# Half of the second channel product's sums into x, moved from VectorE to a ScalarE copy and a GpSimd DMA that adds in SBUF

## The chip, the cores and the metric

The kernel runs on one core of a Trainium2 chip. Its engines are TensorE (PE in the profile), VectorE (DVE), ScalarE (ACT), GpSimd (POOL) and SyncE (SP, which here issues the loads and stores). The metric is device time in microseconds; the median of three runs of the kernel before is 458.24 us (458.11 to 458.42).

## The reference

Three blocks run one after the other on a batch of 2, a sequence of 768 and a width of 512. The first is a linear attention with a decay, of 8 heads:

```
state = gamma * state + k_t v_t^T
y_t   = scale * q_t state
```

The second mixes along the sequence through a rank of 32 and then runs a channel network of width 2048:

```
u   = x + (x^T U V)^T
x   = u + relu(u @ w_ch1) @ w_ch2
```

The third is a gated block, with a normalised half and a 768 x 768 spatial matrix:

```
h      = relu(x @ w_in);  u, v = halves of h
v_s    = w_spatial @ normalise(v) + b_spatial
output = (u * v_s) @ w_out
```

The change touches the second block's last line: the sum of `relu(u @ w_ch1) @ w_ch2` into x.

## The kernel before

x lies in SBUF, feature by token: for each batch b a tile of 128 partitions with 4 feature blocks d and 768 tokens, cut into two halves h of 384. Products are made with three PE instructions each ("triple"): every operand is split into a high part and the low part that is left over (`hw` and `lw` of a weight, `f..` and `a` of data), and high times high, high times low and low times high are added in PSUM.

The channel network goes through the 2048 hidden features in 8 steps m of 256, for each b; `ch1` makes the hidden features of a step and `ch2` multiplies them with the step's rows of w_ch2. `ch2` makes 8 products of 128 x 384 for each (m, b): for h in 0, 1 and d in 0 to 3, two triples into one PSUM bank named acc, which DVE then adds to x (line 760). PE's program runs ch1 of the next (m, b) interleaved with ch2 of this one. In the first two steps (m below MS = 2) ch1 is four plain products (banks c); from the third on it is a Strassen-like scheme of seven (`quad`, banks q), whose operands are differences of blocks of u (`differ`, tiles s0..t, and `split`, tiles f0..t). These differences read x before the sums of ch2 have changed it, so a sum may have to wait for them.

The weights come as 64-bit numbers and are made into float32 by `convert` (two ACT conversions yw and tw, two DVE instructions on rw, one POOL addition on rw) and split by `parts` (ACT cast hw, subtraction lw on DVE or POOL).

Nothing of the order is written by hand. Every piece of work is handed to `Plan.op` with the engines that may do it and a cost for each, the tiles that it reads and writes, and a key (a due time). `arrange` then plays the program through: at each step it takes the operation that can start first by its costs, engine by engine, and fixes its place in that engine's queue; `settle` repeats this in 15 rounds, in which each key is moved half way to the latest start that `latest` works out. So one operation with another engine or cost can shift the order in other places. Tiles come from pools (`POOLS`) with a fixed number of buffers, of which `ps` are PSUM's 8 banks; an operation cannot be placed before there is a buffer. The engines run their queues strictly in that order and wait for each other by semaphores.

Names that the rows use: t are transposes of x, xtok their copies, g and gt the rank-32 product of the second batch and its copy, hu its product with V, which is added to x (line 509).

Of the kernel before, what the change touches and what calls it, by code (L numbers as in the profile page):

```python
# [8 lines left out]
F32 = mybir.dt.float32  # L9
# [12 lines left out]
P = 128  # L22
# [4 lines left out]
T = S // 2  # L27
# [10 lines left out]


class Op:  # L40
    __slots__ = ("key", "eng", "fn", "bufs", "deps", "outs", "need", "start", "end", "seq", "size", "cost")


class Plan:
# [13 lines left out]
        self.ops, self.last, self.readers = [], {}, {}  # L58
        self.key, self.pace = 0.0, 1.0

    def op(self, eng, fn, r=(), w=(), key=None, size=0):

        o = Op()
        o.key, o.eng, o.fn, o.size = (self.key if key is None else key), dict(eng), fn, size
        deps, bufs = {}, []
        for tok in list(r) + list(w):
            b = tok if isinstance(tok, Buf) else tok[0]
            if isinstance(b, Buf) and b not in bufs:
                bufs.append(b)
                b.left += 1  # L70
        for tok in r:
            if tok in self.last:
                deps[self.last[tok].seq] = self.last[tok]
        for tok in w:
            for x in self.readers.get(tok, ()):
                deps[x.seq] = x
            if tok in self.last:
                deps[self.last[tok].seq] = self.last[tok]
        for tok in w:
            self.last[tok] = o  # L80
            self.readers[tok] = []
        for tok in r:
            if tok not in w:
                self.readers.setdefault(tok, []).append(o)
        o.deps = list(deps.values())
        o.key = max([o.key] + [x.key + 1e-6 for x in o.deps])
        o.bufs, o.outs, o.need, o.seq = bufs, [], len(o.deps), len(self.ops)
        for d in o.deps:
            d.outs.append(o)
        self.ops.append(o)  # L90
        return o

    def arrange(self, sizes):
# [54 lines left out]
        while given < len(order):  # L148
            best, moved = None, False
            for e in self.ENGINES:  # L150
                can = []
                for o in cands[e]:
                    t0 = room(o)
                    if t0 is not None:
                        can.append((o.seq, o, t0) + span(o, e, t0))
                if not can:
                    continue
                low = min(c[3] for c in can) + SLACK.get(e, 30.0)
                for _, o, t0, st, en in sorted(can, key=lambda c: c[0]):
                    if st > low:  # L160
                        continue
                    if len(o.eng) > 1:
                        x = min(o.eng, key=lambda x: span(o, x, t0)[1] + BIAS[x] + harm(o, x) + sum(c.eng[x][0] for c in cands[x] if c.seq < o.seq and len(c.eng) == 1 and c.key > o.key - NEAR))
                        for z in [z for z in o.eng if z != x]:
                            cands[z].remove(o)
                            del o.eng[z]
                        moved = moved or x != e
                        if x != e:
                            continue
                    if best is None or st < best[0]:  # L170
                        best = st, en, o, e
                    break
            if best is None and moved:
                continue
            if best is None:
                left = sorted({o.seq: o for e in cands for o in cands[e]}.values(), key=lambda o: o.seq)
                raise RuntimeError("nothing can start: " + "; ".join(f"{o.key:.1f} {[b.name for b in o.bufs]}" for o in left[:5]) + f" {({p: (len(s), [b.name for b in queue[p][head[p]:head[p] + 3]]) for p, s in slots.items()})}")
            st, en, o, e = best
            given += 1
            for x in o.eng:  # L180
                cands[x].remove(o)
            if e in "DE":
                free[e] = st + 430.0
                en = dma = max(st + 1500.0 + o.size / 210.0, dma + o.size / 360.0)
            else:
                free[e] = en
                if e == "P":
                    tiles = o.eng[e][1]
                elif o.eng[e][1]:
                    port = [en - 20.0, e]  # L190
            o.start, o.end, o.cost, o.eng = st, en, o.eng[e], e
            for b in o.bufs:
                if b not in placed:
                    placed.add(b)
                    heapq.heappop(slots[b.pool])
                    while head[b.pool] < len(queue[b.pool]) and queue[b.pool][head[b.pool]] in placed:
                        head[b.pool] += 1
                b.left -= 1
                b.end = max(b.end, en + self.LAG[e])
                if not b.left:  # L200
                    heapq.heappush(slots[b.pool], b.end)
            for x in o.outs:
                x.need -= 1
                if not x.need:
                    add(x)

    def latest(self):

        end = max(o.end for o in self.ops)
        free = {e: end + 1e3 for e in self.ENGINES}  # L210
        tiles, late = None, {}
        for o in sorted(self.ops, key=lambda o: (-o.start, -o.seq)):
            e, cost = o.eng, o.cost
            t = end
            for x in o.outs:
                if e != "P" or x.eng != "P":
                    t = min(t, late[x] - self.LAG[e] - (45.0 if x.eng == "G" and e != "G" else 0.0))
                else:
                    t = min(t, late[x])
            if e in "DE":  # L220
                t = min(t - 1500.0 - o.size / 210.0, free[e] - 430.0)
            else:
                t = min(t, free[e] + self.OVER[e]) - cost[0]
                if e == "P":
                    t -= 130.0 if tiles not in (None, cost[1]) else 0.0
                    tiles = cost[1]
            free[e] = late[o] = t
        return late
# [64 lines left out]

NM = NF // 2

POOLS = {"a": 36, "w": 24, "raw": 2, "y": 2, "t": 2, "r": 6, "st": 6, "s": 2, "g": 2, "sm": 2, "ps": 8}
SLACK = {'P': 0.0, 'V': 100.0, 'A': 150.0, 'G': 300.0, 'D': 30.0}
BIAS = {'V': 0.0, 'G': 0.0, 'A': -200.0}
HARM = 10.0
# [13 lines left out]
INPLACE = lambda m, b, i, h: False  # L313

MS = 2
SEQ = [(m, b) for m in range(NM) for b in range(B)]

STEP = {n: 6 * pe(n)[0] / 1000 for n in (T, DM // 2)}
# [5 lines left out]
def tile_kernel(ctx: ExitStack, tc: tile.TileContext, a, out: bass.AP):  # L324
# [425 lines left out]
    def ch2(m, b):  # L750
        for h in range(2):
            for d in range(ND):
# [3 lines left out]
                for i in range(2):  # L756
                    wh, wl = W["tile", "w2", 2 * m + i]
                    x = A[m, b, i, h]
                    triple(o, i == 0, i == 1, T, lambda wh=wh, sl=sl: wh.t[:, sl], lambda wl=wl, sl=sl: wl.t[:, sl], lambda x=x: x.t[:, 0, :], lambda x=x: x.t[:, 1, :], [wh, wl, (x, 0), (x, 1)])
                op({"V": vps(T)}, lambda E, o=o, v=xs(b, d, h): E.tensor_add(v, o.t, v), r=[o, ("X", b, d, h)], w=[("X", b, d, h)])  # L760

# [279 lines left out]
```

## Time and profile before

| | us |
|---|---|
| median of 3 runs | 458.24 |
| the profiled execution | 458.86 |
| its span, first to last instruction | 457.1 |
| PE busy | 450.3 (99%) |
| DVE busy | 394.8 (86%) |
| ACT busy | 252.7 (55%) |
| POOL busy | 106.6 (23%) |

The granted clock of PE is 1.00 over the span. Matmuls overlap: a 128 x 384 one is listed with 334 ns, but the next starts about 0.17 us after it, so PE that is busy without a gap is PE that starts one after the other. In the timelines a row can hold several instructions of one form in a row ("x2"), and the square bracket at its end says how long the engine stood idle before it and for whom.

### The profile page before, as it was taken

How to read it: one execution, taken by the hardware profiler on the slowest of the kernel's cores; microseconds unless marked ns; L12 is line 12 of the kernel's file. 1: busy time of each engine (PE TensorE's matmuls, PEld its weight loads, DVE VectorE, ACT ScalarE, POOL GpSimd, SP SyncE). 2: the span in 40 equal slices, each digit the busy share in tenths (PEclk: the TensorE clock that was granted, in tenths of full speed). 3: DMA queues.
4: the chain of work that ended last, by engine and by line, in shares of the span. 5: the costliest groups of instructions: out<-in, count | busy, mean ns of one | idle time of the engine just before them, and what ended most of it. 6: DMA issues, size and time to landing. Idle time of an engine off the chain costs nothing.

```text
span 457.1 us, 8432 instructions
## 1 busy us (share of the span) xinstructions
PE 450.3 (99%) x3245; PEld 437.3 (96%) x3245; DVE 394.8 (86%) x836; ACT 252.7 (55%) x518; POOL 106.6 (23%) x100
## 2 busy tenths in 40 slices
PE   9999989999999999999999999999999999999996
PEld 5888869999999999999999999999999999999996
DVE  2766989899998999999789788899998899999943
ACT  2366785635665665666355444557657778443510
POOL 3045454444324221331031012101310001240000
PEclk9999999999999999999999999999999999999999
DMA  8994521412324132334122112100004220000033
GB/s 298 400 397 175 180 93 47 138 47 92 100 87 139 52 133 92 93 93 138 47 74 66 46 47 69 36 1 1 1 1 138 94 93 1 1 2 0 0 139 138
DMA packets 14296, 43.34 MB, mean 95 GB/s; under 512 B 1713, under 2 KB 2609, under 8 KB 14257
## 3 DMA queue, kind: packets, MB, share of 16 engines
q1 hardware_dynamic: 14112, 42.80, 27.6%
q8 instruction: 25, 0.41, 0.4%
q14 instruction: 15, 0.11, 0.1%
q10 hardware_dynamic: 144, 0.02, 0.0%
HBM read 39.67 MB, written 3.15 MB: 94 GB/s over the span
## 4 chain that ended last, share of the span: by engine, by line
PE 95%; DVE 3%; ACT 1%; issue 0%; ACTq 0%
PE acc L336 29%; PE pz L336 11%; PE c L336 7%; PE sc L336 3%; PE x L336 3%; PE idle L336 1%; PE ds L336 1%; DVE x L509 1%; PE t L478 1%; DVE x L462 1%; PE qu11c L336 0%; PE qu11d L336 0%; PE qo11d L336 0%; PE qo11c L336 0%; PE qo11a L336 0%; PE qo10d L336 0%
## 5 line engine op out<-in xcount | busy, mean ns | idle before, releaser
L336 PE MATMUL acc<-a,hw 128*128 128x384 f32 x512 | 129.8, 334 | 0.0
L336 PEld LDWEIGHTS acc<-a,hw 128*128 128x128 f32 x512 | 92.4, 188 | 0.0
L336 PE MATMUL acc<-a,lw 128*128 128x384 f32 x256 | 85.5, 334 | 0.0
L760 DVE TENSOR_TENSOR x<-acc,x 128x384 f32<-128x384 f32 x128 | 69.5, 550 | 8.2 <-PE acc L336 8.0
L576 POOL TENSOR_TENSOR rw<-rw,tw 128x512 int32<-128x512 int32 x32 | 44.1, 1383 | 109.8 <-DVE rw L574 104.2
L336 PEld LDWEIGHTS acc<-a,lw 128*128 128x128 f32 x256 | 48.1, 188 | 0.0
L733 ACT ACTIVATE y<-y 128x384 f32<-128x384 f32 x36 | 18.9, 526 | 40.5 <-DVE y L732 40.4
L571 ACT ACTIVATE yw<-raww 128x512 f32<-128x512 f32 x32 | 21.5, 675 | 18.4 <-DVE rw L574 17.7
L572 ACT ACTIVATE tw<-raww 128x512 int32<-128x512 uint32 x32 | 21.5, 673 | 3.3 <-POOL rw L576 3.3
L735 DVE TENSOR_TENSOR a<-y,a 128x384 fp32r<-128x384 f32 x36 | 20.7, 574 | 2.8 <-ACT a L734 2.4
L574 DVE SCALAR_TENSOR_TENSOR rw<-yw,rw 128x512 uint32<-128x512 uint32 x32 | 22.2, 702 | 0.0
L427 DVE SCALAR_TENSOR_TENSOR pt<-sc,scales,shared 128x384 f32<-128x384 f32 x21 | 12.0, 609 | 9.5 <-PE sc L336 9.5
L336 PE MATMUL pz<-hws,vn 128*128 128x384 f32 x72 | 19.1, 335 | 0.0
L734 ACT CAST a<-y 128x384 fp32r<-128x384 f32 x36 | 18.5, 514 | 1.0
L336 PE MATMUL pz<-ws,vn 128*128 128x384 f32 x108 | 19.0, 334 | 0.0
L336 PEld LDWEIGHTS pz<-ws,vn 128*128 128x128 f32 x108 | 18.8, 188 | 0.0
L585 DVE TENSOR_TENSOR lw<-rw,hw 128x512 fp32r<-128x512 f32 x19 | 17.7, 931 | 0.4 <-ACT hw L584 0.4
L576 POOL TENSOR_TENSOR rwo<-rwo,two 128x512 int32<-128x512 int32 x4 | 5.2, 1293 | 54.8 <-DVE rwo L574 54.8
L336 PE MATMUL c<-f00b,hw 128*128 128x384 f32 x64 | 16.6, 340 | 0.0
L336 PE MATMUL c<-f01b,hw 128*128 128x384 f32 x64 | 16.2, 334 | 0.0
L584 ACT CAST hw<-rw 128x512 fp32r<-128x512 f32 x20 | 12.4, 620 | 5.1 <-POOL rw L576 5.0
L336 PEld LDWEIGHTS sc<-q,k 64*128 64x128 f32 x192 | 12.4, 193 | 2.8 <-issue 1.4
(1007 smaller groups left out, 1242.4 us busy)
## 6 DMA issues: line engine op xcount, KB each, us to landing
raww<-in_w SPq DMA_DIRECT2D x32, 512.0 KB, 3.5
q<-in_qT SPq DMA_DIRECT2D x8, 384.0 KB, 7.9
k<-in_kT SPq DMA_DIRECT2D x8, 384.0 KB, 7.7
kk<-in_k SPq DMA_DIRECT2D x8, 384.0 KB, 7.7
v<-in_v SPq DMA_DIRECT2D x8, 384.0 KB, 7.8
raws<-in_ws SPq DMA_DIRECT2D x6, 384.0 KB, 3.0
out_y<-out SPq DMA_DIRECT2D x6, 384.0 KB, 2.3
rawwu<-in_wu SPq DMA_DIRECT2D x4, 512.0 KB, 3.5
```

Source lines behind the costliest of these rows:

```text
L336: nc.tensor.matmul(o, l, r, start=start, stop=stop, skip_group_check=True)
L427: op({"V": (611, False)}, lambda E, pt=pt, x=sc[e], m=m: E.scalar_tensor_tensor(pt(), x.t, m, tri(), ALU.mult, ALU.mult), r=[sc[e], "sc", ...
L571: op({"A": c}, lambda E: E.activation(y.t, words(1).bitcast(F32), AF.Copy, scale=2.0 ** -112), r=whole, w=[y])
L572: op({"A": c}, lambda E: E.activation(t.t, words(0), AF.Copy, scale=2.0 ** -29), r=whole, w=[t])
L574: op({"V": vss(n)}, lambda E: E.scalar_tensor_tensor(r.t, y.t.bitcast(U32), 0x80000000, r.t, ALU.bitwise_and, ALU.bitwise_or), r=[y, r], w ...
L576: op({"G": gss(n)}, lambda E: E.tensor_tensor(o().bitcast(I32), r.t.bitcast(I32), t.t, ALU.add), r=[r, t], w=[tok])
L584: op({"A": acp(DM)}, lambda E: E.copy(h.t, f(r.t)), r=[r], w=[h])
L585: op({"V": vss(DM), "G": gss(DM)}, lambda E: E.tensor_sub(l.t, f(r.t), f(h.t)), r=[r, h], w=[l])
L733: op({"A": (525, False)}, lambda E: E.activation(y[0](), y[0](), AF.Relu), r=[y[1]], w=[y[1]])
L734: op({"A": acp(T)}, lambda E: E.copy(t.t[:, 0, :], y[0]()), r=[y[1]], w=[(t, 0)])
L735: op({"V": vss(T), "G": gss(T)}, lambda E: E.tensor_sub(t.t[:, 1, :], y[0](), f(t.t[:, 0, :])), r=[y[1], (t, 0)], w=[(t, 1)])
L760: op({"V": vps(T)}, lambda E, o=o, v=xs(b, d, h): E.tensor_add(v, o.t, v), r=[o, ("X", b, d, h)], w=[("X", b, d, h)])
```

## The change

In `ch2`, for all steps but the last (m below 7), the sums of the feature blocks d = 1 and d = 3 are no longer a DVE addition. ACT copies the PSUM bank into an SBUF tile sg (pool of two), and POOL issues a DMA from sg to that part of x which adds to what is there. That is 4 of the 8 sums of each (m, b), 56 in all. The planner counts the DMA with 1000 ns on POOL and with 2500 ns more until its result is there (`tail`). The pool st, of which the quads take their temporary tiles, goes from 6 buffers to 5.

```diff
@@ Plan.op, Plan.arrange, Plan.latest
-    def op(self, eng, fn, r=(), w=(), key=None, size=0):
+    def op(self, eng, fn, r=(), w=(), key=None, size=0, tail=0.0):
...
+            en += o.tail
             o.start, o.end, o.cost, o.eng = st, en, o.eng[e], e
...
-                t = min(t, free[e] + self.OVER[e]) - cost[0]
+                t = min(t - o.tail, free[e] + self.OVER[e]) - cost[0]
...
-POOLS = {"a": 36, "w": 24, "raw": 2, "y": 2, "t": 2, "r": 6, "st": 6, "s": 2, "g": 2, "sm": 2, "ps": 8}
+POOLS = {"a": 36, "w": 24, "raw": 2, "y": 2, "t": 2, "r": 6, "st": 5, "s": 2, "g": 2, "sg": 2, "sm": 2, "ps": 8}
...
+SENT = [(d, h) for d in (1, 3) for h in range(2)]
+SEND = 1000.0, False
...
@@ ch2
-                op({"V": vps(T)}, lambda E, o=o, v=xs(b, d, h): E.tensor_add(v, o.t, v), r=[o, ("X", b, d, h)], w=[("X", b, d, h)])
+                v, tok = xs(b, d, h), ("X", b, d, h)
+                if m < NM - 1 and (d, h) in SENT:
+                    sg = Buf("sg", [P, T], F32, f"sg{m}{b}{h}{d}")
+                    op({"A": aps(T)}, lambda E, o=o, sg=sg: E.copy(sg.t, o.t), r=[o], w=[sg])
+                    op({"G": SEND}, lambda E, sg=sg, v=v: E.dma_start(v, sg.t[:], accum_op=ALU.add), r=[sg, tok], w=[tok], tail=2500.0)
+                else:
+                    op({"V": vps(T)}, lambda E, o=o, v=v: E.tensor_add(v, o.t, v), r=[o, tok], w=[tok])
```

The order of PE's instructions stays nearly as it was (four groups of three change places with a neighbour, and around 55 to 66 us the first c products take their tiles in another order); SP's stays the same; from about 300 us on all five queues are the same. The queues of DVE, ACT and POOL are new between about 54 and 300 us.

The first place is ACT's queue around gt, the copy that PE's product hu reads (c_929 and c_932 are the same first c product of the channel network, x_95 and x_98 batch 0 of x, x_96 and x_99 batch 1). Before:

```order
L571 ACTIVATE yw_960<-raww_847 128x512
L729 ACTIVATE a_989<-c_929 128x384
L537 CAST f00t_992<-s00t_962 128x384
L571 ACTIVATE yw_996<-raww_902 128x512
L465 COPY gt_1000<-g_964 128x128
L584 CAST hw_1008<-rw_885 128x512
```

And with the change:

```order
L574 ACTIVATE yw_958<-raww_850 128x512
L732 ACTIVATE a_993<-c_932 128x384
L574 ACTIVATE yw_997<-raww_905 128x512
L468 COPY gt_999<-g_968 128x128
L587 CAST hw_1007<-rw_888 128x512
```

The cast of f00t, which waits for the difference s00t of DVE, no longer stands ahead of gt.

The second place is DVE's queue from there to lw, the low half of the weight tile with which PE goes on after hu. Before:

```order
L730 SCALAR_TENSOR_TENSOR a_989<-c_929,a_989 128x384
L509 TENSOR_TENSOR x_96<-hu_1002,x_96 128x384
L509 TENSOR_TENSOR x_96<-hu_1003,x_96 128x384
L574 SCALAR_TENSOR_TENSOR rw_994<-yw_960,rw_994 128x512
L585 TENSOR_TENSOR lw_1033<-rw_885,hw_1008 128x512
```

With the change:

```order
L733 SCALAR_TENSOR_TENSOR a_993<-c_932,a_993 128x384
L512 TENSOR_TENSOR x_99<-hu_1001,x_99 128x384
L577 SCALAR_TENSOR_TENSOR rw_965<-yw_958,rw_965 128x512
L588 TENSOR_TENSOR lw_1027<-rw_888,hw_1007 128x512
L512 TENSOR_TENSOR x_99<-hu_1002,x_99 128x384
```

One sum of hu stands behind lw instead of ahead of it.

And PE, directly behind hu, has before:

```order
L336 MATMUL c_1037<-f00b_845,hw_859 128x384
L336 MATMUL c_1037<-f00b_845,lw_889 128x384
L336 MATMUL c_1045<-f00b_683,hw_1008 128x384
L336 MATMUL c_1045<-f00b_683,hw_1008 128x384
L336 MATMUL c_1045<-f00b_683,lw_1033 128x384
```

With the change:

```order
L339 MATMUL c_1037<-f00b_686,hw_1007 128x384
L339 MATMUL c_1037<-f00b_686,hw_1007 128x384
L339 MATMUL c_1037<-f00b_686,lw_1027 128x384
L339 MATMUL c_1037<-f00b_689,hw_1007 128x384 x2
L339 MATMUL c_1037<-f00b_689,lw_1027 128x384
```

The triple with the weight tile that was there already (hw_859, lw_889) has gone further back, so lw is asked for three products earlier.

The third place is POOL's queue where the moved sums begin (steps (0, 0) and (0, 1), 70 to 100 us in the trace of before). With the change:

```order
L767 DMA x_98<-sg_1162 128x384
L579 TENSOR_TENSOR rw_1177<-rw_1177,tw_1033 128x512
L579 TENSOR_TENSOR rw_1182<-rw_1182,tw_1120 128x512
L541 TENSOR_TENSOR f00t_1184<-s00t_1169,f00t_1184 128x384
L767 DMA x_98<-sg_1263 128x384
L579 TENSOR_TENSOR rw_1257<-rw_1257,tw_1224 128x512
L579 TENSOR_TENSOR rw_1280<-rw_1280,tw_1246 128x512
L767 DMA x_98<-sg_1336 128x384
L535 TENSOR_TENSOR s01t_1371<-x_99,s01t_1352 128x384
L767 DMA x_99<-sg_1393 128x384
L767 DMA x_98<-sg_1212 128x384
L767 DMA x_99<-sg_1437 128x384
```

The DMAs stand between the additions of the weight conversion, of which before had these in a row with differences and splits. The DMA of sg_1212, the second copy that ACT makes, comes fifth: it changes a part of x that the planned differences read until then.

## Rows read from the trace of the kernel before

**Rows 1.** Windows: busy us of PE, PEld, DVE, ACT, POOL; PEclk, DMA share, GB/s

```profile
0.00:54.00 54.00, 52.46 (x828) 42.09 (x828) 34.87 (x66) 29.19 (x60) 20.96 (x30) 1.00 0.81 297
54.00:64.00 10.00, 8.32 (x103) 5.96 (x95) 8.89 (x16) 6.99 (x15) 3.65 (x4) 1.00 0.28 78
64.00:292.00 228.00, 228.00 (x1315) 228.00 (x1316) 207.32 (x407) 128.15 (x245) 63.22 (x50) 1.00 0.27 85
292.00:440.00 148.00, 148.00 (x933) 148.00 (x932) 138.11 (x340) 86.46 (x196) 18.77 (x18) 1.00 0.10 34
440.00:457.10 17.10, 13.56 (x79) 13.23 (x77) 5.58 (x10) 1.93 (x4) 0.00 (x0) 0.99 0.32 124
```

**Rows 2.** Line 760: ns min/median/max, first and last start in us

```profile
L760 DVE TENSOR_TENSOR x<-acc,x x128: 541/549/560, 73.6 to 321.8; 128x384 f32<-128x384 f32 x128
```

**Rows 3.** PE's waits over the span: us in total, times, longest

```profile
PE hu L336 <- ACT gt L465: 1.2, 1, 1.2
...
PE c L336 <- DVE lw L585: 0.5, 1, 0.5
```

**Rows 4.** Timeline of PE from 57 us: start, us, instructions, idle before

```profile
57.83 1.52 PE L336 MATMUL g<-xtok,ust 128*32 128x128 f32 x48
...
60.77 1.57 PE L336 MATMUL hu<-vst,gt 32*128 32x384 f32 x16 [1.16 <-ACT gt L465]
...
64.00 0.45 PE L336 MATMUL c<-f00b,lw 128*128 128x384 f32 x1 [0.52 <-DVE lw L585]
```

**Rows 5.** Timeline of ACT, 55 to 61.5 us

```profile
57.98 0.46 ACT L729 ACTIVATE a<-c 128x384 fp32r<-128x384 f32 x1
59.24 0.51 ACT L537 CAST f00t<-s00t 128x384 fp32r<-128x384 f32 x1 [0.80 <-DVE s00t L532]
59.89 0.67 ACT L571 ACTIVATE yw<-raww 128x512 f32<-128x512 f32 x1
60.47 0.25 ACT L465 COPY gt<-g 128x128 f32<-128x128 f32 x1
```

**Rows 6.** Timeline of POOL, 57.2 to 64.5 us

```profile
57.39 1.41 POOL L576 TENSOR_TENSOR rw<-rw,tw 128x512 int32<-128x512 int32 x1 [2.96 <-DVE rw L574]
```

**Rows 7.** Timeline of DVE, 54.5 to 64.5 us

```profile
57.57 1.64 DVE L532 TENSOR_TENSOR s00t<-x 128x384 f32<-128x384 f32 x1
...
61.72 1.02 DVE L509 TENSOR_TENSOR x<-hu,x 128x384 f32<-128x384 f32 x2 [1.10 <-PE hu L336]
62.66 0.68 DVE L574 SCALAR_TENSOR_TENSOR rw<-yw,rw 128x512 uint32<-128x512 uint32 x1
63.26 0.69 DVE L585 TENSOR_TENSOR lw<-rw,hw 128x512 fp32r<-128x512 f32 x1
```

**Rows 8.** Timeline of PE, 68.9 to 70.6 us

```profile
69.48 0.51 PE L336 MATMUL c<-f01b,hw 128*128 128x384 f32 x2
```

**Rows 9.** A costly group of the page: busy us, mean ns, idle before

```profile
L576 POOL TENSOR_TENSOR rw<-rw,tw 128x512 int32<-128x512 int32 x32 | 44.1, 1383 | 109.8 <-DVE rw L574 104.2
```

**Rows 10.** Line 465, the copies of a PSUM bank on ACT

```profile
L465 ACT COPY xtok<-t x13: 462/480/491, 20.4 to 56.9; 128x384 f32<-128x384 f32 x13
```

**Rows 11.** DMA issues: KB each, median us to landing

```profile
q<-in_qT SPq DMA_DIRECT2D x8, 384.0 KB, 7.9
...
out_y<-out SPq DMA_DIRECT2D x4, 192.0 KB, 1.9
bb<-in_bsp SPq DMA_DIRECT2D x2, 192.0 KB, 2.9
```

**Rows 12.** Timeline of PE, 80.3 to 86.3 us, the last matmuls of two products

```profile
80.75 0.33 PE L336 MATMUL acc<-a,lw 128*128 128x384 f32 x1
...
84.91 0.33 PE L336 MATMUL acc<-a,lw 128*128 128x384 f32 x1
```

**Rows 13.** Timeline of PE, 73.5 to 75.3 us, the end of a product

```profile
74.51 0.33 PE L336 MATMUL acc<-a,lw 128*128 128x384 f32 x1
```

**Rows 14.** Timeline of DVE, 82.5 to 83.5 us, its sum

```profile
82.89 1.01 DVE L760 TENSOR_TENSOR x<-acc,x 128x384 f32<-128x384 f32 x2
```

More of the change, by code (lines that the diff above doesn't have):

```diff
@@ L40 @@
 class Op:
-    __slots__ = ("key", "eng", "fn", "bufs", "deps", "outs", "need", "start", "end", "seq", "size", "cost")
+    __slots__ = ("key", "eng", "fn", "bufs", "deps", "outs", "need", "start", "end", "seq", "size", "cost", "tail")
 class Plan:
@@ L86, in op @@
         o.key = max([o.key] + [x.key + 1e-6 for x in o.deps])
-        o.bufs, o.outs, o.need, o.seq = bufs, [], len(o.deps), len(self.ops)
+        o.bufs, o.outs, o.need, o.seq, o.tail = bufs, [], len(o.deps), len(self.ops), tail
         for d in o.deps:
```

## The prediction

> **What bounds the kernel now.** I read the table of windows first. In it the reader is to see that from 64 to 440 us TensorE (PE) is busy the whole time, 228.00 of 228.00 us and 148.00 of 148.00 us, while VectorE (DVE) is busy 91% and 93% of the same stretches [rows 1]. The second channel product, whose sums the change moves, begins in the first of them (its 128 sums start between 73.6 and 321.8 us, 112 of them in the seven steps that the change touches) [rows 2]. So DVE work taken out there is worth nothing by itself: PE is what ends last, and no instruction of PE goes away. PE has room only before 64 us, where 8.32 of 10 us are busy between 54 and 64, and in the tail after 440 us.
>
> Second I read PE's waits. After 54 us two are listed: 1.2 us for a ScalarE (ACT) copy that makes gt, and 0.5 us for a DVE subtraction that makes lw, the low half of a weight tile [rows 3]. The timeline of PE shows both in their place: g ends at 57.83 + 1.52 = 59.35, hu starts only at 60.77, and the c product that needs lw goes on at 64.00 [rows 4]. From there on PE never waits until the tail. A microsecond that PE gains before 64 us is therefore carried to the end, unless the changed work makes PE wait later.
>
> **The change part by part.**
>
> *The order on ACT around gt.* The planner puts everything in a new order, and the first difference that matters lies ahead of the first moved sum. Before, ACT's queue held a cast of f00t in front of gt [rows 5]. That cast waited for s00t on DVE, which took 1.64 us (57.57 to 59.21), because GpSimd's (POOL) addition ran from 57.39 to 58.80 [rows 6, 7]; then came the cast to 59.75, a yw conversion from 59.89 (0.67 us), and only then gt at 60.47. In the changed order the cast is gone from this place: yw, the Relu of a, yw, gt. The Relu ends at 57.98 + 0.46 = 58.44 (its c product is not earlier: the same four triples and four groups of transposes stand ahead of g). The second yw then ends at about 59.1, and gt waits for nothing but g. So gt starts at 59.35 + 0.03 = 59.38, ends 0.25 us later, and hu starts 0.05 us after it, as before (60.72 to 60.77): 59.68 instead of 60.77. That is 1.09 us earlier.
>
> *The order on DVE around lw.* Here DVE now has: first sum of hu, rw, lw; before it had both sums of the first pair, rw, lw. The first sum starts 0.95 us after hu (60.77 to 61.72), one sum takes 0.47 us of the queue, rw 0.60 (62.66 to 63.26), lw 0.69 [rows 7]: 59.68 + 0.95 + 0.47 + 0.60 + 0.69 = 62.39. PE, however, asks for lw sooner than before: at the third product after hu and not at the sixth, because the c product that covered it (with the weight tile that was already there) is moved back. PE goes on at 62.39 + 0.05 = 62.44 with the third product, and reaches the sixth after three products of 0.17 us at 62.95. Before, the sixth went on at 64.00. So the gain that leaves this stretch is 64.00 - 62.95 = 1.05 us: PE still waits for lw, a little longer than before, and that is what is late next.
>
> What lw needs is in time: its rw has an addition on POOL behind an instruction of DVE that stands earlier than before, and the cast hw comes directly behind gt, two microseconds before lw needs it. The f01b operands that PE asks for next (69.48 in the trace [rows 8], about 68.4 now) have their first two subtractions on POOL, which has ahead of them rw (from about 61.7, behind the rw of DVE) and one lw: four instructions of at most 1.38 us [rows 9], done by 67.2.
>
> *The moved sums.* 56 of those 112 sums leave DVE, 56 x 0.55 = 31 us [rows 2]; 56 ACT copies of 0.48 us come in its place [rows 10], 27 us on an engine that is busy 128.15 of 228 us [rows 1]. Both lie beside a PE that is busy throughout: worth 0. If that cover went, 31 us of DVE would be the ceiling, but nothing in the rows has PE waiting on a DVE sum there.
>
> *The 56 DMAs.* No row of before has a transfer issued by POOL or one that adds. Its price on POOL I bound by 0 and by POOL's dearest instruction, 1.38 us [rows 9]; I take 1.38, since POOL has room (63.22 of 228 us). The time to landing I bound by 1.9 us (a store of the same 192 KB) and 7.9 us (loads in the crowded start); I take 2.9 us, the row of the same size that writes into SBUF [rows 11]. By the Trainium skill (DMA: Bandwidth & Descriptors, Anatomy of one DMA — SWDGE (gpsimd) path) one such transfer takes 2.0 us plus its bytes over 436 GB/s, an estimate of 2.45 us here; no run here shows it.
>
> A moved sum thus holds its staging tile sg for 0.48 + 1.38 + 2.9 = 4.76 us. Moved sums come 4.16 us apart (products end at 81.08 and 85.24) [rows 12]. With two tiles that leaves 8.3 us, and nothing waits. In the first two steps one tile is stuck: the DMA of sg_1212 stands fifth in POOL's queue, since it may not change x before the planned differences have read it. There four copies share one tile and run 0.6 us later each, 2.4 us in all. ACT stands still meanwhile, and behind it are casts of weights and operands and the Relu of a. What PE would feel first is a PSUM bank that is not given back. But before, the third product of this stretch, ended at 74.84, was added to x only at about 83.4 (by the order of DVE's queue it is the second of two sums from 82.89) [rows 13, 14]: a bank was held 8.5 us and PE did not wait. So I put 2.4 us of lateness at nothing for PE.
>
> *What else moves.* st has 5 buffers instead of 6; from 300 us on every engine's order is the same as before, and I cost it at 0, with the tail. SP's order is unchanged; its loads wait for ACT's tw, which can come later by the 2.4 us above. I cost that at 0 too; if the weights had less room than that, PE would wait for them, and this belongs to the rival on slow landing.
>
> **Sum.** The profiled execution took 458.86 us (span 457.1 and 1.76 around it): 458.86 - 1.05 = 457.8. It lay 0.62 us above the median of the runs, 458.24, so on that scale 457.2.
>
> **The rivals.**
>
> *Gain not delivered: about 458.2.* The gain rests on two short chains. If the second yw finds its tile not yet loaded, gt stands behind it as before; or if a POOL addition falls on lw as it fell on s00t (1.64 us, where a sum of the same shape takes 0.55), lw comes 1.1 us later and eats the whole. For it: DVE and POOL meet often in these stretches. Against it: in before rw and lw stood in the same succession, with POOL's next addition right behind that rw, and lw took 0.69. A small stall later in the dense stretch ends here too.
>
> *Landing is slow: slower, about 460.* Mechanism: a copy on ACT waits for its sg tile, ACT's queue behind it stops, and PE runs out of banks and operands. In the steady state it decides from 8.3 - 0.48 - 1.38 = 6.4 us of landing; in the first two steps a landing of 5 us makes four copies late by 2.7 us each, 10.8 in all, about 2.3 us beyond the 8.5 that a bank was seen to bear. Less the 1.05 gained that is 459.5; at 6 us 14.8, 6.3 beyond, 463.5. At 7.9 us (the row) every step would take 2 x 9.76 = 19.5 instead of 16.6 us on the way of the copies, 40 us in 14 steps. For it: the transfer reads x as well as sg, so it moves more than the row taken. Against it: the DMA engines are busy 27% of this stretch, against 81% in the start that the 7.9 comes from [rows 1]. DVE, however, is busy 91% of it, and if a transfer had to find its gaps, three times 2.9, or 8.7 us, would be past the 6.4. The Trainium skill speaks against the change here (SBUF — State Buffer, SBUF: two separate sides): descriptors of a DMA issued by GpSimd are written by GpSimd, which cannot write while DVE runs an instruction in a two-port mode, so that such a transfer can take several times as long; no run here shows it.
>
> *More than forecast: about 456.6.* PE's two waits hold 1.68 us, and 54 to 64 us has that much idle. All of it would come back only if lw came 0.5 us sooner.
>
> **How the numbers follow.** About 0.2% (0.9 us) is what a measurement of this kernel tells from no change. Forecast (a gain between 0.5 and 1.4, most of it above 0.9): 0.55, of which 0.40 to faster and 0.15 to the same. Gain not delivered or given back: 0.22, 0.19 to the same and 0.03 to slower. Slow landing: 0.17, 0.15 to slower and 0.02 to the same. More: 0.06, faster. That makes faster 0.46, same 0.36, slower 0.18. The likeliest case's own range is 456.8 to 457.7. The range for 8 in 10: down to 456.5, where PE's waits are all gone; up to 459.3, which takes in the case of no gain and the lower end of slow landing.
>
> **What would show it.** Right: PE's wait for gt falls from 1.2 to about 0.1 us, a wait for lw of 0.5 to 0.9 us remains, the first product with f01b starts near 68.4, and 64 to 440 us stays without a wait on PE; DVE's busy time falls by some 30 us. Wrong: ACT copies at the sg line that wait long for a DMA together with waits of PE on ACT in 85 to 110 us; a landing above 5 us; gt no earlier than 60.

## The result, and the profile after

The changed kernel takes 461.47 us (median of 4 runs, 461.40 to 461.77) against 458.33 for the kernel before (4 runs beside it, 458.11 to 458.64): 1.0069 of it, 95% interval 1.0052 to 1.0087. It is 3.1 us slower; forecast were 457.2 us and a range that ended at 459.3.

The table of windows of the changed kernel, columns as in [rows 1]; the second fence is one more window of the kernel before, the third the same window after:

```profile
54.00:64.00 10.00, 8.75 (x105) 6.76 (x102) 8.53 (x16) 7.45 (x16) 5.49 (x5) 1.00 0.33 100
64.00:292.00 228.00, 226.32 (x1300) 224.82 (x1299) 192.80 (x352) 147.01 (x295) 106.94 (x101) 1.00 0.56 130
292.00:440.00 148.00, 148.00 (x933) 148.00 (x932) 138.94 (x342) 88.28 (x200) 19.45 (x19) 1.00 0.11 34
```

```profile
64.00:155.00 91.00, 91.00 (x525) 91.00 (x526) 86.53 (x169) 54.14 (x105) 35.40 (x29) 1.00 0.30 96
```

```profile
64.00:155.00 91.00, 89.33 (x511) 88.02 (x510) 87.91 (x153) 62.36 (x126) 52.59 (x48) 1.00 0.57 141
```

Two things are to be seen. PE, dense from 64 to 440 us before, now has holes between 64 and 155. And DVE, which lost 22 of its 42 sums in those 91 us (12.1 us at 0.55), is busy longer there than before, 87.91 against 86.53 us. Over 64 to 292 us it won 14.5 us, not the 31 of the forecast.

PE's waits after (columns as in [rows 3]) show who it waits for:

```profile
PE acc L339 <- DVE a L738: 1.0, 2, 0.8
...
PE hu L339 <- ACT gt L468: 0.7, 1, 0.7
...
PE c L339 <- DVE lw L588: 0.5, 1, 0.5
...
PE q20c L339 <- DVE y L675: 0.4, 1, 0.4
PE acc L339 <- ACT a L737: 0.2, 1, 0.2
```

The lines left out lie before 57 us. The waits for gt and lw are those of [rows 3]; the other three are new, and all of them wait for what DVE makes, or for an ACT instruction behind it. Set side by side, matmul by matmul, the two traces say where the time goes: the changed kernel starts 0.28 us later at 8 us (loads), is 0.64 us ahead at hu (60.13 against 60.77) and 0.48 at the product that waits for lw, stays so until 128 us, and falls back in four places: to level at 130.8, then 0.50 behind at 136.6, 0.97 at 137.2 and 2.18 at 154.0. Up to 185 us it grows to 2.46, with no wait listed, and from there the distance stays. The two profiled executions differ by as much, 461.41 against 458.86. Nearly all of the loss, 2.66 of 2.94 us, falls between 128 and 154 us, among the quads of step 2 and the first of step 3.

The new instructions themselves are cheap, as the costliest groups of the page show (columns as in [rows 9]):

```profile
L767 POOL DMA_DIRECT2D x<-sg x56 | 49.4, 882 | 97.3 <-ACT sg L766 90.0
L579 POOL TENSOR_TENSOR rw<-rw,tw 128x512 int32<-128x512 int32 x32 | 46.4, 1464 | 20.9 <-DVE rw L577 19.6
...
L766 ACT COPY sg<-acc 128x384 f32<-128x384 f32 x56 | 26.7, 476 | 12.6 <-PE acc L339 10.0
```

POOL spends 0.88 us on each DMA; from issue to landing the median is 3.2 us, and of ACT's waits for a staging tile there are 2, 1.2 us in all. What has grown is DVE's own work. Groups of POOL's and DVE's lines from 64 to 155 us, before and after:

```profile
L576 POOL TENSOR_TENSOR rw<-rw,tw 128x512 int32<-128x512 int32 x15 | 21.1, 1410 | 37.7 <-DVE rw L574 32.0 <-ACT hw L584 2.9 <-ACT f00t L537 2.7
...
L585 DVE TENSOR_TENSOR lw<-rw,hw 128x512 fp32r<-128x512 f32 x9 | 9.8, 1084 | 0.4 <-ACT hw L584 0.4
L573 DVE TENSOR_SCALAR rw<-yw 128x512 uint32<-128x512 uint32 x15 | 6.5, 441 | 0.0
L538 DVE TENSOR_TENSOR f01t<-s01t,f01t 128x384 fp32r<-128x384 f32 x4 | 2.1, 548 | 0.0
L615 DVE TENSOR_TENSOR lsaw<-saw,hsaw 128x512 fp32r<-128x512 f32 x3 | 2.0, 680 | 0.0
```

```profile
L579 POOL TENSOR_TENSOR rw<-rw,tw 128x512 int32<-128x512 int32 x16 | 22.6, 1412 | 13.4 <-DVE rw L577 12.1 <-ACT tw L575 1.3
...
L588 DVE TENSOR_TENSOR lw<-rw,hw 128x512 fp32r<-128x512 f32 x9 | 10.9, 1214 | 1.2 <-ACT hw L587 1.2
L769 DVE TENSOR_TENSOR x<-acc,x 128x384 f32<-128x384 f32 x20 | 10.7, 544 | 0.0
L576 DVE TENSOR_SCALAR rw<-yw 128x512 uint32<-128x512 uint32 x17 | 9.7, 579 | 0.0
L541 DVE TENSOR_TENSOR f01t<-s01t,f01t 128x384 fp32r<-128x384 f32 x5 | 4.7, 952 | 0.0
L618 DVE TENSOR_TENSOR lsaw<-saw,hsaw 128x512 fp32r<-128x512 f32 x3 | 3.7, 1231 | 0.0
```

POOL's additions take as long as before, 1.41 us. The same instructions of DVE take up to 1.8 times as long on average (lsaw, 680 to 1231 ns). The sums that read a PSUM bank don't: 544 ns, as in [rows 2]. One place shows what changed. Timelines of POOL and of DVE in the kernel before, then in the changed one:

```profile
106.85 2.94 POOL L576 TENSOR_TENSOR rw<-rw,tw 128x512 int32<-128x512 int32 x2 [2.52 <-DVE rw L574]
...
107.29 0.55 DVE L760 TENSOR_TENSOR x<-acc,x 128x384 f32<-128x384 f32 x1
107.89 0.56 DVE L730 SCALAR_TENSOR_TENSOR a<-c,a 128x384 fp32r<-128x384 f32 x1
108.37 0.55 DVE L760 TENSOR_TENSOR x<-acc,x 128x384 f32<-128x384 f32 x1
```

```profile
104.30 1.59 POOL L579 TENSOR_TENSOR rw<-rw,tw 128x512 int32<-128x512 int32 x1
...
104.09 2.23 DVE L541 TENSOR_TENSOR f01t<-s01t,f01t 128x384 fp32r<-128x384 f32 x2
```

Before, two sums and a low part, which read PSUM, run beside POOL's additions at their usual 0.55 us each. After, two subtractions with both operands in SBUF stand beside the addition, and they take 2.23 us where two take some 1.1.

The largest of PE's new waits shows the way from there to PE. POOL, DVE and PE in the changed kernel, then the same instruction of DVE in the kernel before:

```profile
152.25 1.27 POOL L579 TENSOR_TENSOR rw<-rw,tw 128x512 int32<-128x512 int32 x1 [0.47 <-DVE rw L577]
...
152.70 1.23 DVE L738 TENSOR_TENSOR a<-y,a 128x384 fp32r<-128x384 f32 x1
...
153.99 0.45 PE L339 MATMUL acc<-a,hw 128*128 128x384 f32 x1 [0.83 <-DVE a L738]
```

```profile
149.58 0.56 DVE L735 TENSOR_TENSOR a<-y,a 128x384 fp32r<-128x384 f32 x1
```

The low part a that PE waits for takes 1.23 us beside POOL's addition, and 0.56 before. It also starts 3.1 us later than before: DVE had fallen behind ahead of it.

Over all of 64 to 155 us, counted from the records (overlap of DVE's instructions with POOL's additions and subtractions; slow-down is the sum, over DVE's instructions, of their duration less the median of the same instruction with none of POOL's beside it):

| 64 to 155 us | before | after |
|---|---|---|
| POOL's additions and subtractions | 34.7 us | 35.2 us |
| beside them, DVE on PSUM operands | 22.4 us | 13.0 us |
| beside them, DVE on SBUF operands only | 11.2 us | 21.7 us |
| DVE's two-input SBUF instructions: alone, beside | 0.57, 0.96 us | 0.57, 1.19 us |
| DVE's instructions on PSUM: alone, beside | 0.55, 0.55 us | 0.55, 0.55 us |
| DVE's slow-down | 6.1 us | 15.9 us |

So beside POOL's additions DVE's instructions on two SBUF operands are slowed, and those that read PSUM are not. That is the rule of the Trainium skill (SBUF — State Buffer, Who interferes with whom): a DVE instruction with two SBUF inputs contends with a GpSimd instruction that reads SBUF, under an exclusive lock, and one with at most one SBUF input, outside the two-port modes, does not. The trace agrees, by 0.57 against 1.19 us and 0.55 against 0.55; that a lock is behind it no run here shows. TENSOR_SCALAR on rw, with one SBUF input, is slowed too, from 0.42 us alone to 0.97; in which mode it ran no run here shows. The moved sums were the harmless company of POOL's additions. Of the 12.1 us that left DVE, 9.8 (15.9 less 6.1) came back as slow-down, and some more as instructions that the planner now gives DVE: f00t and f01t 11 instead of 9, POOL 5 instead of 7.

### The profile page after: what moved, and what is told of

Same layout as the page of the kernel before. It is cut to its first block, busy times and chain, and to the rows that moved or that the text cites. A ratio compares the mean times of both kernels' runs of the same rounds, so it can differ in the third digit from the quotient of the medians.

```text
span 459.7 us, 8586 instructions
## 1 busy us (share of the span) xinstructions
PE 450.2 (98%) x3245; PEld 436.8 (95%) x3245; DVE 381.7 (83%) x785; ACT 273.4 (59%) x572; POOL 152.2 (33%) x153
## 4 chain that ended last, share of the span: by engine, by line
PE 76%; DVE 17%; DMA 2%; issue 1%; ACT 1%; POOL 0%; SPq 0%; ACTq 0%; DVEq 0%
PE acc L339 21%; PE pz L339 11%; PE x L339 3%; PE c L339 2%; DVE rw L577 2%; DVE rw L576 2%; DVE x L769 2%; PE sc L339 2%; DVE lw L588 2%; DMA v<-in_v 1%; DVE a L733 1%; DVE f00t L541 1%; DVE f01t L541 1%; PE ds L339 1%; DMA raww<-in_w 1%
## 5 line engine op out<-in xcount | busy, mean ns | idle before, releaser
L767 POOL DMA_DIRECT2D x<-sg x56 | 49.4, 882 | 97.3 <-ACT sg L766 90.0
L579 POOL TENSOR_TENSOR rw<-rw,tw 128x512 int32<-128x512 int32 x32 | 46.4, 1464 | 20.9 <-DVE rw L577 19.6
L769 DVE TENSOR_TENSOR x<-acc,x 128x384 f32<-128x384 f32 x72 | 38.8, 547 | 10.4 <-PE acc L339 10.4
L766 ACT COPY sg<-acc 128x384 f32<-128x384 f32 x56 | 26.7, 476 | 12.6 <-PE acc L339 10.0
L577 DVE SCALAR_TENSOR_TENSOR rw<-yw,rw 128x512 uint32<-128x512 uint32 x32 | 25.5, 799 | 0.2
L576 DVE TENSOR_SCALAR rw<-yw 128x512 uint32<-128x512 uint32 x32 | 16.9, 538 | 0.1
L428 POOL TENSOR_TENSOR pt<-pt,shared 128x384 f32<-128x384 f32 x11 | 10.8, 1003 | 17.7 <-ACT pt L427 17.7
```

What stands on the lines that cost most here:

```text
L576: op({"V": vone(n)}, lambda E: E.tensor_single_scalar(r.t, y.t.bitcast(U32), 3, ALU.logical_shift_left), r=[y], w=[r])
L577: op({"V": vss(n)}, lambda E: E.scalar_tensor_tensor(r.t, y.t.bitcast(U32), 0x80000000, r.t, ALU.bitwise_and, ALU.bitwise_or), r=[y, r], w ...
L579: op({"G": gss(n)}, lambda E: E.tensor_tensor(o().bitcast(I32), r.t.bitcast(I32), t.t, ALU.add), r=[r, t], w=[tok])
L766: op({"A": aps(T)}, lambda E, o=o, sg=sg: E.copy(sg.t, o.t), r=[o], w=[sg])
L767: op({"G": SEND}, lambda E, sg=sg, v=v: E.dma_start(v, sg.t[:], accum_op=ALU.add), r=[sg, tok], w=[tok], tail=2500.0)
L769: op({"V": vps(T)}, lambda E, o=o, v=v: E.tensor_add(v, o.t, v), r=[o, tok], w=[tok])
```

## The experiments

Theory A: the order written for sent sums puts POOL's additions beside DVE's SBUF work in a stretch where DVE has no room. Its rivals: the copies, the bytes or the late landing (B to D), and POOL's queue being full and late (E, F). All were timed beside the kernel before, whose median was 458.2 to 458.5. All ratios are to it, with the 95% interval.

| run | what | us | ratio |
|---|---|---|---|
| e1 | changed, copies and DMAs of 8 columns | 460.01 | 1.0036 (1.0023 to 1.0049) |
| e2 | sent in steps 3 to 6 only | 458.76 | 1.0010 (1.0001 to 1.0018) |
| e3 | sent in steps 0 to 2 only | 461.65 | 1.0067 (1.0054 to 1.0081) |
| e4 | changed, short additions on POOL | 457.30 | 0.9975 (0.9966 to 0.9985) |
| e5 | changed, DMAs of 8 columns | 460.91 | 1.0064 (1.0051 to 1.0076) |
| e6 | changed, copies of 8 columns | 460.57 | 1.0055 (1.0043 to 1.0068) |
| e7 | before, gt first | 457.34 | 0.9981 (0.9972 to 0.9990) |
| e8 | before, 24 sums of 8 columns | 458.34 | 1.0000 (0.9990 to 1.0009) |
| e9 | all sent, in place | 467.68 | 1.0204 (1.0190 to 1.0218) |
| e10 | before, short additions on POOL | 457.18 | 0.9974 (0.9963 to 0.9985) |
| e11 | before, gt and lw first | 456.62 | 0.9959 (0.9947 to 0.9972) |
| e12 | changed, three short additions | 457.30 | 0.9978 (0.9968 to 0.9987) |
| e13 | all sent, in place, DMAs later | 458.37 | 1.0002 (0.9993 to 1.0011) |
| e14 | e9 with three short additions | 460.18 | 1.0047 (1.0035 to 1.0060) |
| e15 | changed, five short additions | 457.23 | 0.9980 (0.9971 to 0.9989) |
| e16 | changed, DMAs later | 461.63 | 1.0077 (1.0065 to 1.0090) |
| e17 | e13 with the rows of e11 | 456.62 | 0.9963 (0.9949 to 0.9977) |

### Where the loss is: e2 and e3

```
+ if 3 <= m < NM - 1 and (d, h) in SENT:      # e2
+ if m < 3 and (d, h) in SENT:                # e3
```

> The changed kernel with the sums sent only in steps 3 to 6 (32 of 56 of them), steps 0 to 2 add on VectorE as before, so the order up to some 185 us is close to that of the kernel before. Theory A (a collision in the stretch 64 to 185 us, where VectorE has no slack): no loss and no gain, 458.0 to 458.8, since in the steady stretch VectorE has slack. Theory B (each sent sum costs about 3.1/56 = 0.055 us wherever it is): 458.33 + 32 x 0.055 = 460.1.

> The changed kernel with the sums sent only in steps 0 to 2 (24 of 56), TensorE's order is that of the changed kernel throughout. Theory A: the whole change of time is made by these 24, 461 to 462, with TensorE first about 0.8 us ahead of the kernel before at 64 us and 2.5 us behind from 185 us. Theory B (a price per sent sum): 458.33 + 24 x 0.055 = 459.7.

As theory A has it: 24 early sums make the whole loss, 32 later ones 0.1%. A price for each sent sum is out.

### Copies and transfers: e1, e5, e6

```
- E.copy(sg.t, o.t)                                   # e1, e6
+ E.copy(sg.t[:, 0:8], o.t[:, 0:8])
- E.dma_start(v, sg.t[:], accum_op=ALU.add)           # e1, e5
+ E.dma_start(v[:, 0:8], sg.t[:, 0:8], accum_op=ALU.add)
```

In e6 the staging tiles are two fixed ones, cleared at the start.

> The changed kernel with its order of instructions untouched on every engine, but each of the 56 ScalarE copies into sg and each of the 56 GpSimd DMAs that add into x carries 8 of 384 columns (the other columns of those sums are left out). Theory A (the order that the planner now writes puts VectorE's two-input work and GpSimd's additions of raw weight words beside each other between 64 and 185 us, VectorE falls behind and TensorE waits; the copies and transfers themselves cost nothing): 460.5 to 462, and TensorE still loses about 3 us between 128 and 185 us. Theory B (the bytes of the transfers, or ScalarE's 27 us of copies, delay what TensorE waits for): most of the 3.1 us comes back, 458 to 459.

> The changed kernel, order untouched: ScalarE's 56 copies into sg are whole again, each GpSimd DMA adds 8 of 384 columns of them into x (the other columns of those sums are left out). With copies and DMAs cut together 1.5 us of the 3.1 us came back. Theory C (those 1.5 us are ScalarE's 0.48 us per copy, which put the casts that VectorE's subtractions wait for later): 461 to 461.8. Theory D (they are the 11 MB that the transfers move through SBUF and the later landing): 459.7 to 460.3. The other half of the loss stays in both.

> The changed kernel, order untouched but for two GpSimd memsets at the start: ScalarE copies 8 of 384 columns, and the DMA adds a whole 128x384 tile into x (zeros but for those 8 columns: the rest of those sums is left out), so that the transfers move as many bytes as in the changed kernel. Theory C (copies): 459.7 to 460.3. Theory D (bytes): 461 to 461.8.

Both theories of e1 missed: about half of the loss stays with nearly nothing copied or sent, and DVE's slow-down with it (15.4 us); the rest comes back. Held against the changed kernel, copies and transfers aren't told apart: by the ratios the copies cut alone give back about 0.6 us and the transfers alone 0.2 of the 1.5 of both, with intervals that overlap that of the changed kernel. Held against e1 they are: with short transfers, whole copies (e5) cost 1.3 us, clear of noise, and PE's three new waits are those of the changed kernel again (1.0, 0.4 and 0.2 us), of which e1 has only the first, at 0.8; with short copies, whole transfers (e6) cost 0.9 us, and the intervals just overlap. So the copies hold most of the rest. What the transfers add is less sure: in the changed kernel ACT waits 1.7 us between 64 and 155 us for loads of weights, before and in e1 not at all.

### What moves beside DVE: e4, e10, e12, e15

```
- E.tensor_tensor(o(), r.t, t.t, ALU.add)                        # 128x512
+ E.tensor_tensor(o()[:, 0:32], r.t[:, 0:32], t.t[:, 0:32], ALU.add)   # e4, e10
+ for z in range(3):   # e12; range(5) in e15: columns 32 z to 32 z + 32
```

(The sum for U and V stays whole.)

> The changed kernel, order untouched, with GpSimd's 32 additions of raw weight words done on 32 of 768 columns (the rest of that sum is left out), so that what ran beside them on VectorE has no GpSimd addition next to it, and GpSimd's queue is freed of some 1.4 us each. Theory A: VectorE's two-input instructions between 64 and 155 us come back from means of 1.4 to 1.6 us to about 0.7, TensorE's waits in 128 to 185 us go, 457.0 to 458. Theory B (transfers, or ScalarE's copies): stays at 460.5 to 462.

> The control of the run with short GpSimd additions: the kernel before, order untouched, GpSimd's 32 additions of raw weight words done on 32 of 768 columns (the rest of that sum is left out). If those additions cost the kernel before nothing but before 64 us, it gains no more than what the chain there gives, 457.3 to 458.3, about as the changed kernel with short additions (457.3), so that the two orders are level once the additions are out of the way. If the changed kernel with short additions is faster only because all kernels are, this one lies 3 us below it, at 454 to 455.

> The changed kernel, order untouched; each of GpSimd's 32 additions of raw weight words is replaced by three additions of 32 columns each (the other 416 of 512 columns of that sum are left out), so that GpSimd is held for about as long as before (3 x 0.49 us against 1.46) and its queue runs on the same times, but moves a fifth of the data beside VectorE. Theory A (the loss is what GpSimd's additions do to VectorE's SBUF work beside them): 457.2 to 458.5, near the run with one short addition. Theory E (the loss is that GpSimd's queue is full and its results come late): 460.5 to 462.

> As the run with three short additions, which turned out to hold GpSimd for 0.96 us in all and not for 1.46: now five of 32 columns for each of the 32 additions of raw weight words (352 of 512 columns of that sum are left out), some 5 x 0.32 = 1.6 us, longer than the one whole addition of the changed kernel. Theory A (data that GpSimd moves beside VectorE): 457.2 to 458.5 again. Theory E (GpSimd held, results late): 460.5 or more.

The pair e4 and e10 first: with the additions out of the way the two orders are level, 457.30 and 457.18 us, where they were 3.1 us apart. But a short addition also ends sooner. (The expectations of e4 and e10 speak of 768 columns; the tile has 512.) e15 keeps POOL held: its groups on POOL and DVE from 64 to 155 us, and the window:

```profile
L582 POOL TENSOR_TENSOR rw<-rw,tw 128x32 int32<-128x32 int32 x86 | 27.8, 495 | 4.4 <-DVE rw L577 4.3
...
L594 DVE TENSOR_TENSOR lw<-rw,hw 128x512 fp32r<-128x512 f32 x10 | 7.4, 739 | 3.5 <-ACT hw L593 3.5
...
L624 DVE TENSOR_TENSOR lsaw<-saw,hsaw 128x512 fp32r<-128x512 f32 x3 | 2.1, 700 | 0.0
```

```profile
64.00:155.00 91.00, 91.00 (x527) 91.00 (x526) 82.63 (x158) 64.35 (x130) 55.22 (x118) 1.00 0.59 147
```

POOL's additions fill 27.8 us instead of 22.6 (1.6 us for each five), its queue is fuller than in the changed kernel (55.22 against 52.59 us), and yet lw takes 0.74 us on average (1.08 in the kernel before, 1.21 in the changed one), lsaw is back at 0.70, PE is dense and the loss is gone. DVE's slow-down is some 6 us, as in the kernel before. ACT still waits 1.7 us for staging tiles there, so those waits were not what made the changed kernel slow. Theory E falls: it is the data that POOL reads and writes in SBUF beside DVE, not that POOL is held.

### The removal alone, and the gain alone: e8, e7, e11

```
+ n = 8 if m < 3 and (d, h) in SENT else T            # e8
+ E.tensor_add(v[:, 0:n], o.t[:, 0:n], v[:, 0:n])
+ gts[1].start = cast[0, 0, "t1", 1].start - 0.01     # e7, e11: gt ahead on ACT
+ low["w11"].start, comb["w21"].start = comb["w21"].start, low["w11"].start   # e11
```

> The kernel before, order untouched, in steps 0 to 2 the 24 sums that the change sends are done on VectorE on 8 of 384 columns (the rest of them is left out): the change's removal of VectorE work without its copies, its DMAs and its order. Theory A: nothing to win, since TensorE waited for no VectorE work there, 458.0 to 458.6; the share of GpSimd's additions that run beside two-input SBUF work rises, so VectorE's freed time is less than 24 x 0.45 us. If the removal itself did harm (less PSUM-reading work beside the additions): above 459.

> The kernel before, no sum sent, one row moved: on ScalarE the second copy of gt (128x128) stands ahead of the cast of f00t and of the load conversion yw, as it does ahead of the cast in the changed kernel. The forecast's first step says that this row alone is worth about 1.05 us before 64 us; nothing else moves. If that step is right and TensorE stays dense after it: 457.2 to 457.7. If what the row gives is taken back later by VectorE, which is busy all through 64 to 155 us: 458.1 to 458.5.

> The kernel before, no sum sent, two rows moved: gt ahead on ScalarE as in the run of that name (457.34, 0.88 us won), and on VectorE the low part lw11 ahead of the combination of rw21, for which TensorE waited 0.47 us at 62 us. If TensorE stays dense after it, both gains add: 456.7 to 457.1. If rw21 0.6 us later is waited for, 457.3 or more.

e8: taking the work off DVE while the order stays wins nothing and harms nothing (slow-down 6.8 us). e7: one row on ACT is worth 0.88 us; ACT's and PE's timelines in e7:

```profile
58.57 0.27 ACT L465 COPY gt<-g 128x128 f32<-128x128 f32 x1 [0.98 <-PE g L336]
58.73 0.52 ACT L537 CAST f00t<-s00t 128x384 fp32r<-128x384 f32 x1
59.14 0.68 ACT L571 ACTIVATE yw<-raww 128x512 f32<-128x512 f32 x1
...
56.98 1.52 PE L336 MATMUL g<-xtok,ust 128*32 128x128 f32 x48
58.43 0.34 PE L336 MATMUL idle<-const-bfloat16-1.0 128*128 128x384 bf16 x1
58.89 1.68 PE L336 MATMUL hu<-vst,gt 32*128 32x384 f32 x16
```

hu starts 0.39 us after the end of g (58.50 to 58.89); before there were 1.42 [rows 4]. With lw first too (e11), both waits are gone and 1.66 us won, the 1.68 (1.16 and 0.52) that [rows 4] hold. No version is faster.

### Sent in place: e9, e13, e14, e16, e17

```
- E.tensor_add(v, o.t, v)
+ def send(E, o=o, v=xs(b, d, h)):            # e9: planned as the addition on V
+     sg = pools["sg"].tile([P, T], F32)
+     nc.scalar.copy(sg, o.t)
+     nc.gpsimd.dma_start(v, sg[:], accum_op=ALU.add)
+     # e13, e17 and (in the changed order) e16: this DMA 1.5 us later
```

> All 56 sums of the change go by a ScalarE copy and a GpSimd DMA, but planned as in the kernel before: where its order has the VectorE addition of such a sum, the copy and the DMA are written into ScalarE's and GpSimd's queues at that place. All other instructions stand on the engines and in the order of the kernel before. Theory A (the loss comes from the order and the choice of engines that the planner writes for sent sums, by which GpSimd's additions meet VectorE's work on SBUF operands): 458.0 to 458.8, and VectorE's work beside GpSimd's additions between 64 and 155 us stays as light as before. Theory B (copies, DMAs and their places in the queues of ScalarE and GpSimd cost it wherever they stand): 460 or more.

> The in-place kernel (all 56 sums sent, all else in the order of the kernel before, 467.68 us) with each GpSimd DMA written 1.5 us later in the planned time, behind GpSimd additions that are due meanwhile, so that these don't wait for the ScalarE copy that the DMA waits for. Theory F (in place it is the DMAs at the head of GpSimd's queue that make its additions late, on average 0.52 us after VectorE's part against 0.18, and shift them beside other VectorE work): lag back to 0.2 to 0.3, 459 to 463. If it is the copies in ScalarE's queue or the transfers: 466 or more.

> The in-place kernel with each of GpSimd's 32 additions of raw weight words replaced by three of 32 columns (the rest of that sum is left out): GpSimd's times stay, the data beside VectorE goes. Theory A (what the additions do to VectorE): most of the 9.4 us goes, 458 to 461. Theory F (lateness of GpSimd's results behind waiting DMAs): 465 to 467.5.

> The changed kernel with each GpSimd DMA written 1.5 us later in the planned time. Its order on ScalarE, VectorE and TensorE stays, and between 64 and 155 us only two DMAs change places with additions (nine rows move later on). Its additions follow VectorE's part by 0.09 us on average already, so if the loss is what VectorE's order has beside them, 460.5 to 462. If DMAs that wait at the head of GpSimd's queue are what is lost here as in place: 458 to 460.

> All 56 sums sent, planned in place with the DMAs 1.5 us later (458.37, level with the kernel before), plus the two rows moved ahead that won 1.66 us without sent sums (456.62). If sending is worth nothing where TensorE is dense: 456.4 to 456.9. If sending gives VectorE room that shows: below 456.2. If it uses up what the rows win: 457.5 or more.

e9 went against my expectation by 9 us: the order of the kernel before is not enough. POOL's group of DMAs in e9 and PE's waits:

```profile
L765 POOL DMA_DIRECT2D x<-sg x56 | 49.7, 887 | 107.7 <-ACT sg L764 87.6
```

```profile
PE q20c L337 <- DVE y L673: 3.0, 1, 3.0
PE acc L337 <- DVE x L768: 2.3, 2, 1.3
```

A DMA at the head of POOL's queue waits for its copy (up to 3.6 us), and the additions behind it come late: between 64 and 155 us they start 1.05 us after DVE's part of the word on average (up to 2.74), where before it was 0.27. (The expectations of e13 and e16 give smaller figures for this delay; those here are counted from the records, from the end of DVE's instruction to the start of POOL's.) They meet other work of DVE: the share on SBUF operands rises to 18.2 us and the slow-down to 13.8, with nothing but the 56 sums moved to another engine. But room on DVE is not what e9 lacks: it is busy only 79.12 of those 91 us, and ACT's casts hw wait 9.6 us there for POOL's additions, against 4.2 before. e13 moves only the DMAs: the delay is 0.29 us again, and 9.3 us of 9.4 are gone. PE's waits in e13, in which none from 64 us on is left:

```profile
PE hu L341 <- ACT gt L470: 1.1, 1, 1.1
...
PE sc L341 <- DVE pt L432: 0.5, 1, 0.5
PE c L341 <- DVE lw L590: 0.5, 1, 0.5
```

So all 56 sums can be sent at no cost. DVE's slow-down is still some 9 us in e13, but DVE is busy 81.36 of the 91 us: a slow-down of that size is no loss where DVE has the room for it. In e14 7.5 of the 9.4 us go, but its three short additions also ended sooner (0.96 us for 1.46), so data and lateness aren't told apart in place. In the changed order (e16) the same shift of the DMAs does nothing, as expected: there the additions follow DVE's part by 0.26 us, as before, and it is DVE's own order beside them that costs. e17 says what sending is worth once nothing costs: 456.62, the same as e11 without it.

## Why the prediction was wrong, step by step

*gt and lw: right, a little large.* Forecast were 1.05 us. In the changed kernel hu starts at 60.13, not 59.68, because the second yw on ACT stood ahead of gt and waited for DVE's rw until 59.26. That rw was late by the same collision that cost the rest: two TENSOR_SCALAR ahead of it took 1.85 us (56.73 to 58.58), 0.42 each alone, beside POOL's addition of 56.41 to 57.95. Of the forecast's 1.05 us, 0.76 are there at lw: 0.48 ahead of the kernel before, and the 0.28 of the later start made good. The row of gt alone (e7) gave 0.88 (interval 0.46 to 1.28). A wait for lw of 0.52 us remained, as forecast. The rival "more" rested on the 1.68 us of both waits, and e11 measured 1.66.

*"Both lie beside a PE that is busy throughout: worth 0": this step failed.* The removal alone is worth 0 (e8). What was wrong is that nothing could be lost: from 0.48 us ahead PE fell to 2.46 behind, 2.94 us on a term put at 0. I read 91% of a window of 228 us [rows 1] and took it as room. Cut to 64 to 155 us, DVE was busy 86.53 of 91 us, so it had 4.5 us to spare at most. The forecast also took all 31 us of the sums as time that DVE wins; it won 14.5, since the sums were what ran beside POOL's additions at no cost, and I did not ask that. I had seen the collision itself, s00t at 1.64 us beside POOL's addition [rows 6, 7], and used it only for gt and for one rival, at 1.1 us and once. It happens all through the stretch from 64 to 155 us, with 21.1 us of these additions on POOL before and 22.6 after, and the planner's new order, which I followed only up to 70 us and from 300 on, was costed at nothing between. (st with 5 buffers, costed at nothing too, stands in e13, which is level.)

*The DMAs: right.* POOL's price 0.88 us (taken 1.38, bounds 0 to 1.38), landing 3.2 (taken 2.9). ACT waited 1.2 us for a staging tile, half of the 2.4 allowed for, so the rival on slow landing had the side right, slower, but by luck: its mechanism is not the one that cost the time. The Trainium skill's rule against the change (SBUF — State Buffer, SBUF: two separate sides), by which such a transfer starves while DVE runs a two-port instruction, did not show: eight issues ran beside DVE's TENSOR_SCALAR (in which mode no run shows), took 0.86 to 1.14 us and landed after 3.0 to 5.0, inside the range of all 56 (0.86 to 1.14 and 3.0 to 6.2).

*"A small stall later in the dense stretch ends here too"* was the nearest to it, and of that rival's 0.22 I put 0.03 on slower, where it went.

What stays open: how the 1.5 us that e1 won back split between copies and transfers (e5 and e6 put most of it on the copies), and by which chain a copy of 0.48 us on ACT reaches PE, on top of the slow-down that stayed.

## What to carry to other kernels

Before work is taken off an engine as worth nothing, cut the window to the stretch where that engine is fullest, and ask what its instructions run beside: here those that read PSUM lost nothing beside GpSimd's additions (0.55 us either way), those with two SBUF operands took twice as long on average (1.19 us against 0.57, 2.34 at most), so removing the first kind can leave the engine as busy as it was. A DMA that waits at the head of GpSimd's queue should stand behind the additions that are due meanwhile; in the order of the kernel before its place alone was worth 9.3 us, in the changed order, where the additions were not late, nothing. And try a side effect of a new order by itself: two rows moved by hand gave 1.66 us, and all 56 sent sums nothing.

## What the runs showed of the hardware

A GpSimd DMA that adds 128x384 floats within SBUF takes 0.88 us of GpSimd's time and lands 3.2 us after its issue (median; 3.0 to 6.2 in 56), against the 2.45 estimated in the prediction. TENSOR_SCALAR, with one SBUF input, is slowed beside GpSimd's additions too: 0.42 us alone, 0.97 beside on average, 2.08 at most, between 64 and 155 us. GpSimd's additions of 128x32 are listed with 0.49 us each, but in a row of five they take 0.32 each, since they overlap (86 of them fill 27.8 us in e15).
